# Retention and MLP-Mixer on one core: who picks the copy of an on-chip buffer

## The chip, the cores and the metric

One core of a Trainium2 chip runs the whole kernel in one launch. The metric is device microseconds, the median of several runs. Before the change it is 189.53 us (three runs, 188.84 to 191.23). On the chip, matmul operands are in float16, sums and the residual in float32; input and output are float32.

## The reference

The input is q, k and v of 4 batches, 8 heads, 768 steps and 64 channels, and four weights. A decayed linear attention comes first, and a mixer block on its output:

```python
state = gamma * state + k_t (outer) v_t          # per batch and head
y_t   = scale * q_t @ state
x     = y, heads side by side                    # 4 x 768 x 512
h     = relu(x^T @ w_tok1) @ w_tok2              # mixes the 768 steps, 256 wide
u     = x + h^T
out   = u + relu(u @ w_ch1) @ w_ch2              # mixes the 512 channels, 1536 wide
```

## The kernel before

The work is cut into operations (class `Op`), each a short run of instructions of one engine, about 1,300 in all. A **front** of a batch `b` and a pair of heads `p` (16 of them) does the attention and the token mixing. It loads q, k and v through POOL's queue (`load`, L494 and L497), scales k and q by the decay into the buffers `k16` and `q16` (`decayed`, L535 on ACT, L537 on DVE), and turns them to `kT` and `qT` (`turn`). In batches 0 and 1 the turning is done by TensorE (L559, L561); in batches 2 and 3 it is done by transposing DMAs of SP's queue (L549, and L785 for `uT`), which read `k16`, `q16` and `u16`. Then come the chunk states (L591, buffer `U` at L601 and L603, buffer `rz` at L621), the scores (L642), the masked scores `am` (L653), the outputs (L673, L699), the evacuation to `x16`, `u16` and `X` (L715), and the two token matmuls (L730, L750). A **back** of a batch widens to 1536 (`widen` L829, `widen7` L898) and narrows to 512 (`narrow` L974, `narrow7` L1048 and L1058). `widen7` and `narrow7` form seven products where eight would be the plain count; they keep partial sums in the buffer `us` (L909, L1038), which DVE adds later (L918, L1065), and sums of operands in `hs`. Output rows leave from `X` by SP's and ACT's queues (L989, L1091).

The **order** of every engine is a fixed list in the source (`ORDERED`), and so is the engine of each operation that could go to two (`WAYS`). The planner `arrange` walks these lists with a cost of each operation and a model of the DMA queues, and gives each operation a start. The program is written in the order of these starts. Three other things hang on the planned times: which of the 8 PSUM banks each accumulator gets, in what sequence the engines' streams are interleaved in the program, and how many filler matmuls (L1173, on zeros) TensorE runs in planned pauses before 21 us.

A buffer in SBUF has a number of copies (`BUFS`): 4 of k, q, v, `kT`, `qT` and `x16`, 3 of `k16`, `u16`, `rz` and `X`, 8 of `am`, 5 of `h1`, 2 of `q16`, `U`, `uT`, `h2`, `hs` and `us`, and one of `late`. An operation that opens a buffer (its `takes`) must wait until all users of the tile that had the copy before are done. Before the change, the planner lets such an operation wait for the oldest tile of the buffer, in the order of taking:

```python
q = taken[s.tag]
k = len(q) - BUFS[s.tag] + ...
x = slot_free(q[k])
```

but it doesn't say which copy is meant. The tile is asked for under the buffer's name with `bufs=BUFS[tag]`, and the allocator of the language picks a copy. Only `rz`, whose tiles are three standing constants, goes round in the order of writing (`made`). PSUM banks are chosen otherwise: the planner takes, of the banks that the operation may have, the one whose last tile is planned to be free first (`room`), and asks for it by its own name (`bank0` to `bank7`).

The planner's model of a transposing DMA, which a step below uses, has a first delay, 48 units and a landing:

```python
FIRST = dict(SP=600, POOL=1800, ACT=700)
return 1600 if t < 115000 else 900       # land(), for op.dma[0] == 48
..., [dst], [src], dma=(48, 28))         # turn(), mode "x"
```

Of the kernel before, what the change touches and what calls it, by code (L numbers as in the profile page):

```python
# [10 lines left out]
F16 = mybir.dt.float16  # L11
# [86 lines left out]
F_ON = 21000  # L98
# [2 lines left out]
FREE = dict(PE=300, ACT=2500, DVE=900, POOL=900, SP=750)  # L101


def arrange(ops, BUFS, BANKS, seq, ways):


    INF = 1e18
    n = len(ops)
    end, start, eng = [None] * n, [None] * n, [None] * n
    begun = [False] * n  # L110
    rings = Rings()
    free = dict(FREE)
    taken = {t: [] for t in BUFS}
    bank_slot = {i: None for i in range(8)}
    lanes, turns = [], []
    line = {e: [] for e in ENGINES}
    for i in seq:
        line[ops[i].ways[ways[i]][0]].append(ops[i])
    at = dict.fromkeys(ENGINES, 0)
    order = []  # L120
    tiled = ""
    t = 0.0

    def slot_free(s):
        m = 0
        for u in s.users:
            x = end[u.n]
            if x is None:
                return INF
            if x > m:  # L130
                m = x
        return m + SEM

    def ready(o, e):
        m = 0
        if o.behind is not None and not begun[o.behind.n]:
            return INF
        for d in o.after:
            x = end[d.n]
            if x is None:  # L140
                return INF
            if x > m:
                m = x
        for d in o.deps:
            if not begun[d.n]:
                return INF
            if end[d.n] is None:
                return INF
            if eng[d.n] == e and e == "PE":
                x = start[d.n]  # L150
            else:
                x = end[d.n] + (25 if eng[d.n] == e and d.dma is None else SEM) + o.guard
            if x > m:
                m = x
        return m

    def room(o):
        m, banks = 0, []
        for s in o.takes:
            if s.tag in BANKS:  # L160
                best = None
                for i in BANKS[s.tag]:
                    if i in banks or i == 7 and t < F_ON:
                        continue
                    x = 0 if bank_slot[i] is None else slot_free(bank_slot[i])
                    if best is None or x < best[0]:
                        best = (x, i)
                if best[0] >= INF:
                    return INF, None
                banks.append(best[1])  # L170
                m = max(m, best[0])
            else:
                q = taken[s.tag]
                k = len(q) - BUFS[s.tag] + sum(1 for s2 in o.takes[:o.takes.index(s)] if s2.tag == s.tag)
                if k >= 0:
                    x = slot_free(q[k])
                    if x >= INF:
                        return INF, None
                    m = max(m, x)
        return m, banks  # L180

    def lane(o, e):
        if o.dma is None or e == "POOL" or len(lanes) < 8:
            return 0
        x = end[lanes[-8].n]
        if x is None:
            return INF
        x += SEM
        if o.dma[0] == 48 and len(turns) > 2:
            y = end[turns[-3].n]  # L190
            if y is None:
                return INF
            x = max(x, y - 900)
        return x

    left = n
    while left:
        moved = False
        wake = INF
        for e in ENGINES:  # L200
            if free[e] > t:
                wake = min(wake, free[e])
                continue
            if at[e] >= len(line[e]):
                continue
            o = line[e][at[e]]
            r = ready(o, e)
            if r > t:
                wake = min(wake, r)
                continue  # L210
            m, banks = room(o)
            m = max(m, lane(o, e))
            if m > t:
                wake = min(wake, m)
                continue
            at[e] += 1
            way = o.ways[ways[o.n]]
            s_ = t
            if e == "PE":
                if o.tiled != tiled:  # L220
                    s_ = max(t, free[e] + (INTO if o.tiled else 0) + (OUT_OF if tiled == "high" else 0))
                tiled = o.tiled
            start[o.n], eng[o.n], begun[o.n] = s_, e, True
            free[e] = s_ + way[1]
            if o.dma:
                for d, x in rings.add(e, o, t):
                    end[d.n] = x
                if e != "POOL":
                    lanes.append(o)
                    if o.dma[0] == 48:  # L230
                        turns.append(o)
                if e == "SP":
                    free[e] = max(t + way[1], rings.made["SP"][-3])
            else:
                end[o.n] = s_ + way[2]
            for i, s in zip(banks, [s for s in o.takes if s.tag in BANKS]):
                bank_slot[i] = s
            for s in o.takes:
                if s.tag not in BANKS:
                    taken[s.tag].append(s)  # L240
            order.append((o, e, way, banks))
            left -= 1
            moved = True
            wake = min(wake, free[e])
        if moved:
            continue
        nxt = min(wake, rings.event)
        for d, x in rings.advance(nxt):
            end[d.n] = x
        if nxt >= INF:  # L250
            raise RuntimeError(f"the plan is stuck at {t}: {left} left")
        t = max(nxt, t + 1) if nxt <= t else nxt
    while rings.event < INF:
        for d, x in rings.advance(rings.event):
            end[d.n] = x
    for o, e, way, banks in order:
        for i, s in zip(banks, [s for s in o.takes if s.tag in BANKS]):
            s.bank = i
    return max(x for x in end), order, start, end

# [46 lines left out]
def kernel(  # L307
# [12 lines left out]
    B, H, S, D = q.shape  # L320
    P = 128
    NC = S // P
# [11 lines left out]
    const_p = ctx.enter_context(tc.tile_pool(name="const", bufs=1))  # L334
    sb = ctx.enter_context(tc.tile_pool(name="sb", bufs=1))
# [2 lines left out]

    BUFS = dict(late=1, k=4, q=4, v=4, k16=3, q16=2, kT=4, qT=4, U=2, r16=2, rz=3, am=8, X=3, x16=4, h1=5, u16=3,
                uT=2, h2=2, hs=2, us=2)  # L340
    BANKS = dict.fromkeys(("first", "front", "back", "back0", "last"), range(8))
    SEVEN = (0, 1, 2, 3)
    SPLIT = (0,)
    WIDE7 = (1, 2, 3,)
# [12 lines left out]
    ops = []  # L357

    def tile_of(slot, shape, dtype):
        if slot.tag == "rz":  # L360
            slot.tile = cross[made[0] % len(cross)]
            made[0] += 1
        elif slot.bank is not None:
            slot.tile = ps.tile(shape, dtype, name=f"bank{slot.bank}", bufs=1)
        else:
            slot.tile = sb.tile(shape, dtype, name=slot.tag, bufs=BUFS[slot.tag])
        return slot.tile


# [26 lines left out]
    ident16 = const_p.tile([P, P], F16, name="ident16")  # L396
    mask = const_p.tile([P, 1, P], FP, name="mask")
    zero = const_p.tile([P, 384], F16, name="zero")
    cross, made = [const_p.tile([P, NC - 1, 2, D], F16, name=f"cross{i}") for i in range(BUFS["rz"])], [0]
    g128 = [(1.0 - 2.0 ** (-5.0 - h)) ** P for h in range(H)]  # L400

    def prep(eng, cost, emit, deps=(), prio=(-20, 0, -1), takes=(), uses=()):
# [23 lines left out]
    def emit():  # L426
        nc.gpsimd.iota(tile_of(SINCE, [P, HC, P], FP), pattern=[[0, HC], [1, P]], base=-MID, channel_multiplier=0,
                       allow_small_or_imprecise_dtypes=True)
# [8 lines left out]
    def emit():  # L437
        gq = tile_of(LATE, [P, NP, SH], FP)
        for p in range(NP):
            nc.scalar.activation(gq[:, p], SINCE.tile.rearrange("p i t -> p (i t)"), AF.Exp, bias=lnsc, scale=lnh[:, p:p + 1])  # L440
# [668 lines left out]
    for what in ORDER:  # L1109
        n = int(what[1:2])  # L1110
# [7 lines left out]
        elif what[0] == "a":  # L1118
            f = CF[n]
# [36 lines left out]
    seq = [digit[a] * 62 + digit[c] for a, c in zip(ORDERED[::2], ORDERED[1::2])]  # L1156
    asked = set(o.n for o in queue)
    asked = [ops[i] for i in seq if i in asked]
    for i, o in enumerate(asked[6:]):
        o.after.append(asked[i])  # L1160
    total, order, start, end = arrange(ops, BUFS, BANKS, seq, [int(x) for x in WAYS])
    for o in ops:
        o.start, o.end = start[o.n], end[o.n]
    nc.vector.memset(zero, 0.0)
# [41 lines left out]
```

## Time and profile before

| | |
|---|---|
| median of three runs | 189.53 us (188.84 to 191.23) |
| the profiled execution | 188.35 us, of which the span of the instructions is 186.6 us |
| TensorE (PE) busy | 178.5 us, 96% of the span, 2093 matmuls |
| VectorE (DVE) busy | 169.6 us, 91%, 464 instructions |
| ScalarE (ACT) busy | 134.7 us, 72%, 306 instructions |
| GpSimd (POOL) busy | 53.7 us, 29%, 63 instructions (mostly issues of loads) |
| granted TensorE clock | full in all 40 slices but for rounding |

"Busy" is the time in which at least one instruction of the engine runs. The idle time before an instruction is put down to what released it. A row of a view by line names the engine, the line in the code, the tile written and the tiles read. Numbers of buffers are left out in these names, so that `k` there may be the loaded k or the buffer `k16` (the row `k<-k,gk` writes `k16` from k), and every PSUM bank is `bank`.

### The profile page before, as it was taken

What the parts mean: (1) busy time and instruction counts of PE and PEld (TensorE: products, weight loads), DVE (VectorE), ACT (ScalarE), POOL (GpSimd) and SP (SyncE); (2) the same over time, 40 slices, a digit from 0 to 9 for tenths busy, and PEclk for the clock granted to TensorE, in tenths of its full rate; (3) what the DMA queues carried; (4) which work ended last, traced back from release to release, by engine and by line L of the source; (5) the groups of instructions that cost most, each with busy time, mean ns of one, the idle gap of its engine ahead of it and who ended that gap; (6) DMA issues with size and microseconds to landing.
All of it is one profiled execution on the core that took longest, in us unless ns stands there. A gap on an engine that the chain in (4) does not pass through costs nothing.

```text
span 186.6 us, 5303 instructions
## 1 busy us (share of the span) xinstructions
PE 178.5 (96%) x2093; PEld 134.7 (72%) x2093; DVE 169.6 (91%) x464; ACT 134.7 (72%) x306; POOL 53.7 (29%) x63
## 2 busy tenths in 40 slices
PE   7888999999999999999999999999999999999990
PEld 3456888656779988866678899767678985566890
DVE  6599898979989998998999999999899999989981
ACT  5749898566899799999999798897983416562210
POOL 8995856544524606506040200000000000000000
PEclk9999999999999999999999999999999999999999
DMA  6999999999999999999999699270019136300053
GB/s 116 160 161 181 197 168 203 197 188 204 161 154 151 144 119 179 130 130 127 161 152 128 178 129 218 42 163 4 0 56 168 34 102 243 152 0 0 4 212 127
DMA packets 92249, 24.92 MB, mean 134 GB/s; under 512 B 81984, under 2 KB 89280, under 8 KB 92224
## 3 DMA queue, kind: packets, MB, share of 16 engines
q0 software_dynamic: 67728, 13.18, 92.7%
q1 hardware_dynamic: 23200, 9.57, 26.6%
q10 hardware_dynamic: 1296, 1.84, 3.2%
q8 instruction: 16, 0.26, 0.6%
q14 instruction: 9, 0.07, 0.1%
HBM read 26.74 MB, written 6.29 MB: 177 GB/s over the span
## 4 chain that ended last, share of the span: by engine, by line
PE 76%; DMA 8%; POOL 6%; ACT 5%; DVE 2%; issue 1%; POOLq 0%; ACTq 0%
PE bank L898 21%; PE bank L1048 14%; PE bank L1058 10%; PE bank L829 7%; PE bank L750 5%; DMA wt<-in_moe_w_tok_dram 4%; PE bank L730 4%; DMA kT<-k 3%; PE bank L642 3%; PE bank L974 3%; PE bank L673 2%; POOL v L497 2%; PE bank L699 2%; POOL k L497 2%; ACT h L845 1%; PE bank L795 1%
## 5 line engine op out<-in xcount | busy, mean ns | idle before, releaser
L653 DVE TENSOR_TENSOR am<-bank,mask 128x384 f16<-128x384 f32 x64 | 33.1, 553 | 2.2 <-PE bank L642 2.2
L918 DVE TENSOR_TENSOR h<-bank,us 128x384 f16<-128x384 f32 x54 | 29.0, 556 | 1.1 <-PE bank L898 0.7
L909 ACT COPY us<-bank 128x384 f32<-128x384 f32 x49 | 22.5, 485 | 9.2 <-PE bank L898 7.7
L497 POOL DMA_DIRECT2D v<-in_v_dram x16 | 16.4, 1023 | 38.9 <-PE bank L699 17.8
L898 PE MATMUL bank<-hs,late 128*128 128x384 f16 x108 | 22.3, 326 | 0.0
L1038 ACT COPY us<-bank 128x256 f32<-128x256 f32 x30 | 11.0, 374 | 14.6 <-PE bank L1048 12.8
L1048 PEld LDWEIGHTS <-hs 128*128 128x128 f16 x198 | 18.5, 98 | 2.5
L1065 DVE TENSOR_TENSOR X<-X,bank 128x256 f32<-128x256 f32 x44 | 17.7, 419 | 1.1 <-PE bank L1058 0.7
L898 PEld LDWEIGHTS <-late 128*128 128x128 f16 x144 | 13.0, 98 | 7.3 <-DVE hs L868 0.4
L621 ACT ACTIVATE cross<-U,gp 64x320 f16<-64x320 f32 x31 | 17.3, 560 | 1.1 <-DVE U L603 0.6
L829 PE MATMUL bank<-uT,wc 128*128 128x384 f16 x96 | 17.7, 326 | 0.0
L1048 PE MATMUL bank<-wsum,hs 128*128 128x256 f16 x132 | 17.6, 273 | 0.0
L497 POOL DMA_DIRECT2D k<-in_k_dram x15 | 15.3, 1022 | 7.9 <-ACT k L535 3.9
L603 DVE SCALAR_TENSOR_TENSOR U<-U,gp,bank 128x64 f32<-128x64 f32 x64 | 17.0, 278 | 0.6
L535 ACT ACTIVATE k<-k,gk 128x384 f16<-128x384 f16 x23 | 13.8, 623 | 3.7 <-DMA k<-in_k_dram 2.4
L845 ACT ACTIVATE h<-bank 128x384 f16<-128x384 f32 x24 | 11.1, 493 | 6.7 <-PE bank L829 6.5
L898 PE MATMUL bank<-uT,wc 128*128 128x384 f16 x72 | 15.8, 326 | 0.0
L715 ACT CAST u<-bank 128x384 f16<-128x384 f32 x32 | 15.1, 484 | 0.9 <-PE bank L750 0.8
L750 PE MATMUL bank<-h,wt 128*128 128x128 f16 x192 | 15.4, 219 | 0.1
L898 PEld LDWEIGHTS <-wc 128*128 128x128 f16 x108 | 10.1, 98 | 5.9 <-issue 0.4
L715 ACT CAST x<-bank 128x384 f16<-128x384 f32 x29 | 13.4, 488 | 0.9 <-PE bank L699 0.9
L1058 PEld LDWEIGHTS <-h 128*128 128x128 f16 x132 | 12.5, 98 | 1.8
(90 smaller groups left out, 390.6 us busy)
## 6 DMA issues: line engine op xcount, KB each, us to landing
out_dram<-X SPq DMA_DIRECT2D x17, 256.0 KB, 2.5
q<-in_q_dram POOLq DMA_DIRECT2D x16, 192.0 KB, 7.7
v<-in_v_dram POOLq DMA_DIRECT2D x16, 192.0 KB, 7.1
k<-in_k_dram POOLq DMA_DIRECT2D x15, 192.0 KB, 8.3
wc<-in_moe_w_ch_dram POOLq DMA_DIRECT2D x5, 512.0 KB, 13.3
out_dram<-X ACTq DMA_DIRECT2D x6, 256.0 KB, 2.2
wc<-in_moe_w_ch_dram POOLq DMA_DIRECT2D x2, 256.0 KB, 9.6
us<-in_k_dram SPq DMA_DIRECT2D x1, 384.0 KB, 3.6
```

The costliest lines, as they stand in the source:

```text
L497: (nc.sync if hard else nc.gpsimd).dma_start(out=tile_of(s, [P, 2, NC, D], FP if hard else F16), in_=src.rearrange("h (c p) d -> p (h c) d ...
L621: nc.scalar.activation(r, u, AF.Copy, scale=g)
L653: nc.vector.tensor_tensor(am, SC[g].tile[:, :m * P].rearrange("p (i t) -> p i t", t=P), mask.to_broadcast([P, m, P]), ALU.mult)
L715: (nc.scalar.copy if e == "ACT" else nc.vector.tensor_copy)(tile(), t)
L750: nc.tensor.matmul(Y[j].tile[:, 2 * i * D:2 * (i + 1) * D], wt2[:, jt, t], H1.tile[:, jt], start=False, stop=(jt == NJ - 1), skip_group_ch ...
L829: nc.tensor.matmul(acc[:, :SH], wc1[:, ct, ft * P:(ft + 1) * P], UT.tile[:, ct, sh * SH:(sh + 1) * SH], start=(ct == 0), stop=(ct == NP - 1))
L898: nc.tensor.matmul(acc[:, :SH], left(ct), r[:, ct], start=first and ct == 0, stop=ct == C2 - 1, skip_group_check=True)
L909: (nc.scalar.copy if e == "ACT" else nc.vector.tensor_copy)(ks[:, j], R1.tile[:, :SH])
L918: nc.vector.tensor_tensor(h(m, sh), R.tile[:, :SH], KS.tile[:, j], ALU.add)
L1048: nc.tensor.matmul(acc_[:, lo], l[:, j], r[:, j], start=first and j == 0, stop=j == K2 - 1, skip_group_check=True)
L1058: nc.tensor.matmul(acc_[:, lo], l[:, j], r[:, j], start=first and j == 0, stop=j == K2 - 1, skip_group_check=True)
L1065: (nc.vector if e == "DVE" else nc.gpsimd).tensor_tensor(dst(), dst(), b_(), ALU.add)
```

## The change

Each copy of each SBUF buffer gets an identity of its own beside the banks: `BANKS` now maps every buffer to a range of numbers from 8 up. The planner chooses among them by the rule of the banks, the copy that it plans to be free first, in place of the wait for the oldest tile. The tile is asked for by a name of its own (`k16_21`, say) with one copy, so nothing is left to the allocator. The three tiles of `rz` are picked by the same number instead of going round. The lists of order and of engines, and all operations, stay as they are.

```diff
-def arrange(ops, BUFS, BANKS, seq, ways):
+def arrange(ops, BANKS, seq, ways):
...
-    taken = {t: [] for t in BUFS}
-    bank_slot = {i: None for i in range(8)}
+    bank_slot = {i: None for ids in BANKS.values() for i in ids}
...
         for s in o.takes:
-            if s.tag in BANKS:
-                best = None
-                for i in BANKS[s.tag]:
...
-            else:
-                q = taken[s.tag]
-                k = len(q) - BUFS[s.tag] + sum(1 for s2 in o.takes[:o.takes.index(s)] if s2.tag == s.tag)
-                if k >= 0:
-                    x = slot_free(q[k])
-                    if x >= INF:
-                        return INF, None
-                    m = max(m, x)
+            best = None
+            for i in BANKS[s.tag]:
+                if i in banks or i == 7 and t < F_ON:
+                    continue
+                x = 0 if bank_slot[i] is None else slot_free(bank_slot[i])
+                if best is None or x < best[0]:
+                    best = (x, i)
+            if best[0] >= INF:
+                return INF, None
+            banks.append(best[1])
+            m = max(m, best[0])
...
-    BANKS = dict.fromkeys(("first", "front", "back", "back0", "last"), range(8))
+    BANKS, ids = dict.fromkeys(("first", "front", "back", "back0", "last"), range(8)), 8
+    for tag, n in BUFS.items():
+        BANKS[tag], ids = range(ids, ids + n), ids + n
...
         if slot.tag == "rz":
-            slot.tile = cross[made[0] % len(cross)]
-            made[0] += 1
-        elif slot.bank is not None:
+            slot.tile = cross[slot.bank - BANKS["rz"][0]]
+        elif slot.bank < 8:
             slot.tile = ps.tile(shape, dtype, name=f"bank{slot.bank}", bufs=1)
         else:
-            slot.tile = sb.tile(shape, dtype, name=slot.tag, bufs=BUFS[slot.tag])
+            slot.tile = sb.tile(shape, dtype, name=f"{slot.tag}_{slot.bank}", bufs=1)
```

More of the change, by code (lines that the diff above doesn't have):

```diff
@@ L159, in room @@
         for s in o.takes:
-            if s.tag in BANKS:
-                best = None
-                for i in BANKS[s.tag]:
[L163 to L168, printed above, removed]
-                    return INF, None
-                banks.append(best[1])
-                m = max(m, best[0])
-            else:
-                q = taken[s.tag]
-                k = len(q) - BUFS[s.tag] + sum(1 for s2 in o.takes[:o.takes.index(s)] if s2.tag == s.tag)
-                if k >= 0:
-                    x = slot_free(q[k])
-                    if x >= INF:
-                        return INF, None
-                    m = max(m, x)
+            best = None
[9 more added lines that the diff above has]
+            m = max(m, best[0])
         return m, banks
@@ L235, in arrange @@
                 end[o.n] = s_ + way[2]
-            for i, s in zip(banks, [s for s in o.takes if s.tag in BANKS]):
+            for i, s in zip(banks, o.takes):
                 bank_slot[i] = s
-            for s in o.takes:
-                if s.tag not in BANKS:
-                    taken[s.tag].append(s)
             order.append((o, e, way, banks))
@@ L256, in arrange @@
     for o, e, way, banks in order:
-        for i, s in zip(banks, [s for s in o.takes if s.tag in BANKS]):
+        for i, s in zip(banks, o.takes):
             s.bank = i
@@ L398 @@
     zero = const_p.tile([P, 384], F16, name="zero")
-    cross, made = [const_p.tile([P, NC - 1, 2, D], F16, name=f"cross{i}") for i in range(BUFS["rz"])], [0]
+    cross = [const_p.tile([P, NC - 1, 2, D], F16, name=f"cross{i}") for i in range(BUFS["rz"])]
     g128 = [(1.0 - 2.0 ** (-5.0 - h)) ** P for h in range(H)]
@@ L1160 @@
         o.after.append(asked[i])
-    total, order, start, end = arrange(ops, BUFS, BANKS, seq, [int(x) for x in WAYS])
+    total, order, start, end = arrange(ops, BANKS, seq, [int(x) for x in WAYS])
     for o in ops:
```

## The prediction

> **What bounds the kernel now.** I read the page's first part, then the windows (busy time of each engine by stretch), then who TensorE waited for, then the chain that ended last, and last the timeline around the one wait for a copy that this chain goes through.
>
> ```profile
> span 186.6 us, 5303 instructions
> PE 178.5 (96%) x2093; PEld 134.7 (72%) x2093; DVE 169.6 (91%) x464; ACT 134.7 (72%) x306; POOL 53.7 (29%) x63
> ```
>
> ```profile
> core 0: us, PE busy (x) PEld busy (x) DVE busy (x) ACT busy (x) POOL busy (x), PEclk, DMA share, GB/s
> 0.00:20.00 20.00, 16.98 (x220) 10.21 (x221) 15.73 (x65) 14.13 (x26) 16.51 (x24) 1.00 1.65 158
> 20.00:58.00 38.00, 37.70 (x506) 28.49 (x506) 34.47 (x76) 29.72 (x69) 21.39 (x25) 1.00 1.84 182
> 58.00:78.00 20.00, 19.88 (x302) 17.53 (x301) 18.91 (x52) 18.69 (x44) 8.07 (x9) 1.00 2.16 144
> 78.00:98.00 20.00, 19.82 (x215) 13.21 (x213) 19.37 (x59) 19.07 (x46) 6.68 (x7) 1.00 2.02 142
> 98.00:120.00 22.00, 21.79 (x293) 19.02 (x291) 21.90 (x61) 19.84 (x48) 1.01 (x1) 1.00 1.02 143
> 120.00:165.00 45.00, 44.98 (x426) 32.93 (x421) 42.77 (x112) 28.24 (x67) 0.00 (x0) 1.00 0.37 98
> 165.00:182.30 17.30, 17.30 (x150) 13.31 (x148) 16.07 (x44) 5.00 (x12) 0.00 (x0) 1.00 0.18 66
> 182.30:186.60 4.30, 0.04 (x1) 0.00 (x0) 0.42 (x1) 0.00 (x0) 0.00 (x0) 0.98 0.28 105
> ```
>
> TensorE sets the time. From 20.0 to 182.3 us it is idle for 0.30 + 0.12 + 0.18 + 0.21 + 0.02 = 0.83 us in all (length less PE busy, row by row). The 3.0 us before 20 us are a wait for first loads, and the 4.3 us behind 182.3 us are the last add and its transfer. Among what TensorE waited for after 20 us no line has more than 0.2 us:
>
> ```profile
> PE bank L591 <- ACT uT L801: 0.2, 1, 0.2
> PE bank L1048 <- DVE h L918: 0.2, 1, 0.2
> PE bank L898 <- DVE h L918: 0.2, 1, 0.2
> ```
>
> A busy PE could still be a slow one. The chain's long pieces answer that (start, length, matmuls):
>
> ```profile
> 124.32 2.65 PE bank L898 x16
> ...
> 134.05 2.60 PE bank L898 x16
> ...
> 154.01 10.99 PE bank L898 x66
> ```
>
> These are 166, 163 and 167 ns a matmul of 384 columns: the same pace wherever one follows the other, so inside the pieces there is nothing to win, and only the seams between them hold more. One more row of the windows, for the last of these pieces (PE busy, then PEld busy):
>
> ```profile
> 154.00:165.00 11.00, 11.00 (x68) 6.36 (x66) 10.45 (x26) 6.78 (x15) 0.00 (x0) 1.00 0.44 168
> ```
>
> The Trainium skill (Perfetto Trace Analysis, "Identifying the Most-Contended Engine") says that matmul busy time does not tell how far TensorE is from its roofline, and that the share of weight loads should be read instead. By that rule the 72% of PEld would leave over a quarter of the span open, and copies that come free earlier could take some of it. The trace does not bear it out here: from 154.01 to 165.00 us matmuls run at 167 ns each without a gap, though weight loads fill 6.36 of these 11.00 us. What this rule would give is the third rival below.
>
> **The change part by part.** No instruction is added, removed or moved to another engine, and each engine's order stays. So every term is a wait that changes its end, or a bank that changes its number.
>
> *Copies whose last reader is always one engine.* The last readers of `v` and `am` are L673 on PE, of `x16` L730, of `h1` L750, of `kT` L642, of `qT` and `rz` L699, all on PE; of `us` they are adds on DVE (L918, L1065); of `U` the scaling at L621, on ACT but for one. One engine's order is fixed, so these copies come free in the same order in the plan and on the chip, whatever the clock. The first planned to be free is then the first that is free. The waits for copies that the trace shows are of this sort:
>
> ```profile
> POOL v L497 <- PE bank L699: 17.8, 4, 5.9
> POOL v L497 <- PE bank L673: 9.9, 2, 9.2
> ...
> ACT us L1038 <- DVE X L1065: 1.8, 1, 1.8
> ...
> ACT us L909 <- DVE h L918: 0.8, 2, 0.5
> ```
>
> Behind POOL's wait for `v` stand the later loads of q, k and v, but TensorE waits for no load after 20 us (rows above). These 27.7 us are hidden by TensorE's work; without that cover, a late load would show as a PE wait at L591. ACT's waits for `us`, 2.6 us, hold up ACT's next evacuations. The copy waited for is the first to come free already, so I take 0 for all of these; bounds: −2.6 if I am wrong about `us` and all of it is on the path, and 0 above, since a copy freed in fixed order can't be picked later.
>
> *Copies with readers on several engines.* These are `k16`, `q16`, `u16`, k and q: in batches 2 and 3 a transposing DMA is among the last readers. One such take waited badly:
>
> ```profile
> 52.74 0.62 ACT k L535
> ...
> 58.62 6.17 DMA kT<-k
> 65.06 0.35 issue
> 65.41 0.35 ACT us L1038
> ```
>
> ```profile
> 57.43 0.32 DVE L537 TENSOR_SCALAR k<-k,gk 128x384 f16<-128x384 f16 x1
> ...
> 60.47 0.51 PE L591 MATMUL bank<-v,k 128*64 128x64 f16 x20
> ...
> 61.19 0.31 DVE L537 TENSOR_SCALAR k<-k,gk 128x384 f16<-128x384 f16 x1
> ...
> 64.89 0.62 ACT L535 ACTIVATE k<-k,gk 128x384 f16<-128x384 f16 x1 [1.18 <-DMA kT<-k]
> ...
> 65.58 0.23 PEld L642 LDWEIGHTS <-kT 64*128 64x128 f16 x8 [0.21 <-issue]
> ...
> 66.10 0.15 PEld L642 LDWEIGHTS <-kT 64*128 64x128 f16 x4 [0.30 <-issue]
> ```
>
> `k16` has three copies, opened at 52.74, 57.43 and 61.19. The next take, at 64.89, waited 1.18 us for the DMA that reads the second, though the first, of batch 1 and read by PE alone, had its last reader end at 60.98 (the row at 60.47). The allocator gave it the wrong one. Which one will the plan give? By the constants of its model a transposing DMA lands 0.60 + 48 × 0.028 + 1.60 = 3.5 us after its issue if nothing else moves, so 62.2 us at the earliest here, and later under POOL's loads. That is behind 60.98, so the plan should take the first copy, and the wait of 1.18 us goes away. Queued behind it on ACT are the `us` evacuation at 65.41 and others that TensorE wants; what TensorE shows of it are the two pauses of its weight loads, 0.21 + 0.30 = 0.51 us, and little idle time of its own. Bounds: 0 and −1.18 us. I take −0.3, nearer to the 0.12 us that PE is idle from 58 to 78 us. DVE is late next: it is busy 18.91 of 20 us there and 21.90 of 22 us from 98 on, so part may be given back.
>
> *Banks dealt anew.* Where the old rule waits for the oldest tile and another is free earlier, the planned times move, by little, and from there on the banks may be dealt out otherwise. A bank dealt badly costs TensorE the rest of an eviction:
>
> ```profile
> L653 DVE TENSOR_TENSOR am<-bank,mask 128x384 f16<-128x384 f32 x64 | 33.1, 553 | 2.2 <-PE bank L642 2.2
> L918 DVE TENSOR_TENSOR h<-bank,us 128x384 f16<-128x384 f32 x54 | 29.0, 556 | 1.1 <-PE bank L898 0.7
> ```
>
> The old deal leaves TensorE 0.83 us of idle time, so the bounds are −0.8 and, for four bad takes at a whole eviction, 4 × 0.556 = +2.2 us. The rule that deals them is unchanged, hence 0.
>
> *Start, end, addresses.* In the first 20 us nearly every copy is used for the first time, so no choice differs, and the 3.0 us and the fillers stay:
>
> ```profile
> L1173 PE MATMUL bank<-zero 128*128 128x384 f16 x35 | 9.1, 400 | 1.1 <-DVE zero L1164 1.1
> ```
>
> If a start did shift, a filler fewer or more is hidden by the wait for loads. The tail's 4.3 us has no copy to wait for. Other addresses cost 0: 64 writes of `am` into eight copies differ by 21 ns at most:
>
> ```profile
> L653 DVE TENSOR_TENSOR am<-bank,mask x64: 544/552/565, 8.8 to 135.2; 128x384 f16<-128x384 f32 x64
> ```
>
> **Sum.** 186.6 − 0.3 = 186.3 us of span. The profiled execution took 188.35 us, 1.75 us more than its span, so it would take 188.05. The median of the three runs is 189.53, 1.18 us above the profiled execution, and on that scale I predict 189.53 − 0.3 = **189.2 us**. That is no change by the measure of 2% (3.8 us), about what a measurement of this kernel can tell.
>
> **The rivals.**
>
> *Nothing moves at all (189.5 us).* The plan picks what the allocator picked, at 64.89 us too. For it: nearly all orders of release are fixed. Against it: the wait of 1.18 us, which the plan's own constants avoid.
>
> *Slower: the plan trusts its landing times.* The copies read by transposing DMAs are freed in the plan by a model (3.5 us alone, 2.8 us after 115 us). The trace has, from issue to landing:
>
> ```profile
> kT<-k SPq DMA_TRANSPOSE x8, 5.5
> qT<-q SPq DMA_TRANSPOSE x8, 3.4
> uT<-u SPq DMA_TRANSPOSE x8, 3.1
> ```
>
> For `k16` the chip is up to 2.0 us later than the model alone. If the plan then hands out a copy that a DMA still reads, ACT or DVE stands at the head of its queue, evacuations behind it are late, and TensorE finds no bank. Priced by the one such wait shown, 1.18 us, all of it on the path, it decides (3.8 us) from the fourth time on: 189.53 + 4.72 = 194.3 us; three times give 193.1. Against it: such a wait cost TensorE far less than 1.18 us here, and under POOL's loads the model slows these DMAs as well.
>
> *Faster: the copies' waits were all on the path.* The waits for copies on ACT are 1.18 + 1.8 + 0.8 = 3.8 us; if all go and TensorE gains all, 189.5 − 3.8 = 185.7 us. Against it: TensorE's idle time is 0.83 us.
>
> **How the numbers follow.** Forecast 0.50, nothing moves 0.20, slower rival 0.22 (0.17 of it beyond 2%), faster rival 0.08 (0.06 beyond). So faster 0.06, within 2% 0.77, slower 0.17. The range goes down by the visible idle time and the whole `k16` wait, 189.53 − 0.83 − 1.18 = 187.5, and up to three bad takes, 189.53 + 3.54 = 193.1; that leaves out the far part of both outer rivals.
>
> **What would show it.** Right: the wait of ACT L535 for the DMA `kT<-k` is gone, POOL's waits for `v` are as long as before, PE is idle under 1 us from 20 us on, fillers are the same 35 and the last matmul ends near 182 us. Wrong: new waits of ACT or DVE for `DMA kT<-k`, `qT<-q` or `uT<-u` at L535, L537 or L715, PE waits for L653 or L918 of half a microsecond, or PE idle time in a stretch that had none; or a start that differs in its first 20 us.

## The result and the profile after

The changed kernel takes 189.04 us (median of 20 runs, 187.73 to 190.72), the kernel before, run beside it, 190.0 us (20 runs, 188.73 to 191.29). The ratio is 0.9938, with a 95% interval from 0.9912 to 0.9965: faster by 0.6%, or 1.2 us (0.7 to 1.7). By the measure of 2% this is no change.

Read side by side, the two programs have the same instructions in the same order on every engine, the same 35 fillers, and the same bank for each of the 268 accumulators. The differences are 30 of the 64 takes of `am`, which exchange copies, two neighbouring takes of `k16`, the addresses, and one more semaphore instruction of ACT. (Lines of the kernel after are 12 lower from `load` on: L535 is L523, L549 is L537, L642 is L630, L898 is L886.)

The page's head and the windows of the profile after, with the same columns as before:

```profile
span 187.8 us, 5304 instructions
PE 178.1 (95%) x2093; PEld 134.7 (72%) x2093; DVE 170.2 (91%) x464; ACT 134.5 (72%) x306; POOL 53.6 (29%) x63
```

```profile
58.00:78.00 20.00, 19.41 (x298) 17.20 (x296) 18.94 (x54) 19.16 (x45) 8.55 (x9) 1.00 2.09 139
78.00:98.00 20.00, 19.14 (x206) 12.63 (x205) 18.93 (x55) 17.59 (x43) 6.11 (x7) 1.00 1.95 141
98.00:120.00 22.00, 21.79 (x290) 19.20 (x288) 21.90 (x62) 19.87 (x49) 1.37 (x2) 1.00 1.06 149
120.00:165.00 45.00, 44.99 (x434) 33.01 (x432) 42.84 (x113) 28.68 (x69) 0.00 (x0) 1.00 0.37 98
```

The faster kernel has the longer span here, 187.8 us against 186.6. One execution is a draw: this one took 189.6 us, above its median, and the profile of before was of an execution of 188.35 us, well below its own. So the two can't be subtracted, and the sections below read each wait in several executions.

The wait for a copy is gone. ACT's timeline around it, after:

```profile
62.98 0.61 ACT L523 ACTIVATE q<-q,gy 128x384 f16<-128x384 f16 x1
63.50 0.46 ACT L703 COPY X<-bank 128x384 f32<-128x384 f32 x1
63.86 0.61 ACT L523 ACTIVATE k<-k,gk 128x384 f16<-128x384 f16 x1
64.38 0.36 ACT L1026 COPY us<-bank 128x256 f32<-128x256 f32 x1
65.29 0.38 ACT L727 ACTIVATE h<-bank 128x256 f16<-128x256 f32 x1 [0.55 <-PE bank L718]
```

The scaling of k follows at once, and ACT now waits for TensorE a little later instead (0.55 us at L727): it has run ahead. The waits for `v` and `us` are as before:

```profile
POOL v L485 <- PE bank L687: 18.0, 4, 6.5
...
POOL v L485 <- PE bank L661: 10.1, 2, 9.1
...
ACT us L1026 <- DVE X L1053: 1.8, 1, 1.8
...
ACT us L897 <- DVE h L906: 0.8, 2, 0.5
```

What made this execution long are two losses that the profile of before did not have:

```profile
76.83 0.51 PE L630 MATMUL bank<-qT,kT 64*128 64x128 f16 x12 [0.59 <-DMA kT<-k]
...
87.22 0.81 DVE L525 TENSOR_SCALAR q<-q,gy 128x384 f16<-128x384 f16 x1 [0.84 <-DMA qT<-q]
...
88.54 0.81 PE L886 MATMUL bank<-hs,late 128*128 128x384 f16 x4 [0.47 <-DVE h L906]
```

At 76.8 us the scores wait until a turned k has landed. At 87.2 us DVE waits to write a copy of `q16` that a transposing DMA still reads; the add behind it in DVE's queue is late, and TensorE waits for its bank.

### The profile page after: what moved, and what is told of

The parts are those of the page before. It is cut to its first block, busy times and chain, and to the rows that moved or that the text cites. A ratio compares the mean times of both kernels' runs of the same rounds, so it can differ in the third digit from the quotient of the medians.

```text
span 187.8 us, 5304 instructions
## 1 busy us (share of the span) xinstructions
PE 178.1 (95%) x2093; PEld 134.7 (72%) x2093; DVE 170.2 (91%) x464; ACT 134.5 (72%) x306; POOL 53.6 (29%) x63
## 4 chain that ended last, share of the span: by engine, by line
PE 74%; DMA 9%; ACT 7%; POOL 5%; DVE 3%; issue 1%; POOLq 0%
PE bank L886 20%; PE bank L1036 13%; PE bank L1046 10%; PE bank L817 7%; PE bank L738 5%; DMA v<-in_v_dram 5%; PE bank L718 5%; DMA kT<-k 4%; PE bank L962 3%; PE bank L630 2%; PE bank L661 2%; POOL k L485 2%; POOL v L485 2%; PE bank L579 2%; PE bank L687 1%; ACT h L833 1%
## 5 line engine op out<-in xcount | busy, mean ns | idle before, releaser
L886 PE MATMUL bank<-hs,late 128*128 128x384 f16 x108 | 22.5, 326 | 0.5 <-DVE h L906 0.5
L886 PEld LDWEIGHTS <-late 128*128 128x128 f16 x144 | 13.0, 98 | 8.0 <-issue 0.9
L886 PE MATMUL bank<-uT,wc 128*128 128x384 f16 x72 | 15.8, 326 | 0.0
L523 ACT ACTIVATE k<-k,gk 128x384 f16<-128x384 f16 x23 | 13.7, 618 | 2.2 <-DMA k<-in_k_dram 2.1
L886 PEld LDWEIGHTS <-wc 128*128 128x128 f16 x108 | 10.1, 98 | 6.1 <-issue 0.6
```

The costliest lines, as they stand in the source:

```text
L886: nc.tensor.matmul(acc[:, :SH], left(ct), r[:, ct], start=first and ct == 0, stop=ct == C2 - 1, skip_group_check=True)
```

## The experiments

### Which part of the change it is

Every ratio here is to the kernel before, run beside the kernel in question, with its 95% interval. Two kernels split the change. In the first, only `k16` is named and chosen by the plan:

```diff
-            slot.tile = sb.tile(shape, dtype, name=f"{slot.tag}_{slot.bank}", bufs=1)
+            own = slot.tag == "k16"
+            slot.tile = (sb.tile(shape, dtype, name=f"{slot.tag}_{slot.bank}", bufs=1) if own else
+                         sb.tile(shape, dtype, name=slot.tag, bufs=BUFS[slot.tag]))
```

> Only k16 is taken from the change: its three copies are named and chosen by the plan, all other buffers are left to the allocator as before. Against the kernel before, two takes of k16 swap copies (the one that waited 1.18 us for the transposing DMA and the next one) and nothing else moves. Theory (this one take is the whole gain): ratio 0.994, between 0.991 and 0.997, ACT's wait for DMA kT<-k at the scaling line is gone. Rival (the gain comes from the new addresses of all copies or from the 30 takes of am that differ): ratio 1.000, though that wait is gone.

Measured: 0.9956 (0.9924 to 0.9987), and the scaling of k (L525 in both of these kernels) follows without a wait:

```profile
64.29 0.61 ACT L525 ACTIVATE k<-k,gk 128x384 f16<-128x384 f16 x1
```

The second has `own = slot.tag != "k16"`.

> The change without k16: all other copies are named and chosen by the plan, k16 is left to the allocator, which gives the take at 64.9 us the same copy as before. Theory (the k16 take is the whole gain): ratio 1.000, between 0.997 and 1.003, and the ACT wait of about 1.2 us for DMA kT<-k is back. Rival (addresses or am): ratio 0.994.

Measured: 1.0016 (0.9989 to 1.0043), and the wait is back in its profile, shorter than in the profile of before:

```profile
65.86 0.62 ACT L525 ACTIVATE k<-k,gk 128x384 f16<-128x384 f16 x1 [0.72 <-DMA kT<-k]
```

So addresses and the 30 takes of `am` are worth nothing that can be measured, and the choice of a copy for `k16` is worth the gain, as far as these intervals can tell. A third kernel gets the same without any naming: the kernel before, with `k16=4` in place of `k16=3`.

> The kernel before, with a fourth copy of k16 and the allocator as before. 13 of 16 takes get another copy, none of them one that a DMA still reads. Theory (the wait for the copy, not who names it, is what counts): ratio 0.994, the same as the change, and no ACT wait for DMA kT<-k. Rival (the plan's names or addresses count): ratio 1.000.

Measured: 0.9932 (0.9906 to 0.9958), without an ACT wait for `DMA kT<-k`. Who names the copy does not matter; that no DMA still reads it does.

### More copies of other buffers

The wait at 87.2 us above is for one of two copies of `q16`. The changed kernel with `q16=3`:

> The changed kernel with a third copy of q16; banks, order and everything else are as in the changed kernel. In the profile after, DVE waits 0.8 us at the scaling of q for DMA qT<-q, near 86 us, for one of the two copies, and TensorE is 0.63 and 0.2 us later after it than in the profile before. Theory (takes that wait for a transposing DMA are what is left): that wait is gone and the ratio to the kernel before is 0.991, so 0.003 below the change alone. Rival (what follows is late anyway since the turned q itself lands late): the wait is gone and the ratio stays at 0.994.

Measured: 0.9927 (0.9902 to 0.9952), with no wait of DVE for `DMA qT<-q`. That is the lowest ratio of all, but its interval holds the change alone (0.9938), so whether the third copy of `q16` adds to it is not settled. The same third copy in the kernel before:

> The kernel before with a third copy of q16, k16 left as it was, with its bad take. The profiles show 0.15 to 0.5 us of TensorE's time for the bad take itself, and the change gained about 1 us, so half a microsecond is not yet found. In two of ten profiles a turned q landed late, near 87 us, DVE waited for a copy of q16 until then, and TensorE lost 0.85 us. Theory (the bad take makes such a late landing more frequent, and that is the rest): ratio to the kernel before 0.997, and no loss near 88 us in its profile. Rival (that event has nothing to do with it and is rare): 1.000.

Measured: 0.9986 (0.9959 to 1.0013). The interval holds both expectations. Its profile has the bad take (one of a copy that a transposing DMA still reads), 1.2 us of wait, and no loss near 88 us.

A third copy of `us`, with a third of `q16`, paid for by `x16=2` and `h1=2`:

> The changed kernel with a third copy of q16 and a third of us, paid for by two copies of x16 in place of 4 and two of h1 in place of 5. Order, banks and fillers are the same. ACT's waits for us at the evacuations (1.8 and 0.8 us in both profiles) should go. Theory (what TensorE waits for after 20 us are no longer copies of us): ratio to the kernel before 0.992, the same as with the third q16 alone, though these waits are gone. Rival (they are on the path): 0.986 or below. If x16 or h1 are now short: above 0.995, with new waits of ACT at their evacuations.

Measured: 0.9959 (0.9932 to 0.9986). No gain from it is seen. The wait of 0.8 us is gone, but the longer of the two waits that were to go is still there:

```profile
ACT us L1026 <- DVE X L1053: 1.8, 1, 1.8
```

So this wait was never for a copy of `us`; the prediction had read it as one. ACT's timeline in this kernel shows what it is:

```profile
178.37 0.34 ACTq L977 DMA_DIRECT2D out_dram<-X  x1
178.75 0.37 ACT L1026 COPY us<-bank 128x256 f32<-128x256 f32 x1 [1.77 <-DVE X L1053]
```

ACT's queue has to issue an output transfer first, whose last add on DVE ended at 178.33 us, and the evacuation follows. The kernel before has the same pair at 176.93 and 177.31 us. The ratio lies above 0.995, where the expectation put it if `x16` or `h1` were short, but the waits that would go with that are not there: ACT's waits at their evacuations are all for TensorE's banks. The interval also holds the change alone (0.9938).

### What a bad take costs

The kernel before, unchanged, has four more profiles (its second to fifth), and the kernel after a second one.

> The kernel before, unchanged, profiled once more. Its first profile is one of its fastest executions (188.35 us against a median near 190), so the wait of 1.18 us in it may be a short one. Theory (the wait lasts until the transposing DMA lands, which differs from execution to execution, and TensorE pays what exceeds about 0.85 us): the wait of ACT for DMA kT<-k near 65 us is 1.0 to 2.5 us here, and TensorE's stretch from 800th to 850th matmul, 4.39 us in the first profile and 4.05 without the wait, is 4.05 plus the wait less 0.85. Rival (the wait is always about 1.2 us and the rest of the 1.0 us gained comes from elsewhere): 1.1 to 1.3 us, stretch 4.4.

> The changed kernel, unchanged, profiled once more. In its first profile two stretches were long that no copy of k16 explains: TensorE waited for DMA kT<-k at 76 us (+0.66 us) and was late again at 88 us (+0.85 us). Theory (these are late transposing DMAs of that execution): at least one of them is gone here. Rival (the change causes them): both are there again. ACT's wait for DMA kT<-k near 64 us is absent under both.

> The kernel before once more, as in the other look at it. Theory: wait of ACT for DMA kT<-k between 0.5 and 2.5 us, and not the same as in the two other profiles; TensorE's stretch from the 800th to the 850th matmul follows it, 4.05 plus the wait less 0.85. Rival: 1.1 to 1.3 us again, 4.4.

> The kernel before, unchanged, one more profile. Theory: the wait of ACT for DMA kT<-k is 0.7 to 1.5 us, and TensorE loses the wait less 0.85 us where it is behind it, 0.14 us shortly after, and in some executions 0.4 us near 76 and 0.85 us near 88 us. Rival: no loss beyond the first two.

> As the look before it: one more profile of the kernel before, with the same two expectations.

The waits of ACT for `DMA kT<-k` in the second to the fifth profile of the kernel before:

```profile
ACT k L535 <- DMA kT<-k: 1.0, 1, 1.0
```

```profile
ACT k L535 <- DMA kT<-k: 0.9, 1, 0.9
```

```profile
ACT k L535 <- DMA kT<-k: 0.5, 1, 0.5
```

```profile
ACT k L535 <- DMA kT<-k: 0.6, 1, 0.6
```

What TensorE pays is seen at its next scores. In the first profile of before, then in the second profile of after (each row has start, length, and at its end the number of matmuls):

```profile
65.58 0.84 PE L642 MATMUL bank<-qT,kT 64*128 64x128 f16 x12
66.36 1.49 PE L1048 MATMUL bank<-wsum,hs 128*128 128x256 f16 x12
```

```profile
65.76 0.51 PE L630 MATMUL bank<-qT,kT 64*128 64x128 f16 x12
66.20 1.48 PE L1036 MATMUL bank<-wsum,hs 128*128 128x256 f16 x12
```

From the scores to the next group it is 0.78 us with the wait and 0.44 without it: 0.34 us lost. The table does this for every matmul. It compares the times from start to start with those of the second profile of after, and gives what is longer by over 0.06 us (times in us; the last matmul is the 2093rd; the run is the sum of the two columns behind it and 6.3, within 0.04).

| kernel, its profile | run | start of the 226th matmul | from there to the last | ACT waits for `DMA kT<-k` | TensorE longer, at |
|---|---|---|---|---|---|
| before | 188.35 | 20.45 | 161.62 | 1.2 | 0.34 at 66; 0.16 at 68 to 71 |
| before, profile 2 | 188.84 | 20.86 | 161.69 | 1.0 | 0.23 at 34; 0.20 at 66; 0.15 at 68 to 71 |
| before, profile 3 | 189.17 | 21.64 | 161.24 | 0.9 | 0.15 at 68 to 71 |
| before, profile 4 | 189.23 | 21.85 | 161.10 | 0.5 | none |
| before, profile 5 | 188.66 | 21.00 | 161.37 | 0.6 | 0.25 at 29 |
| before with three `q16` | 189.28 | 21.09 | 161.89 | 1.2 | 0.25 at 29; 0.37 at 66; 0.15 at 68 to 71 |
| all but `k16` | 190.48 | 21.90 | 162.31 | 0.7 | 0.36 at 76; 0.85 at 87 to 89 |
| after | 189.60 | 20.74 | 162.58 | none | 0.66 at 76; 0.85 at 87 to 89 |
| after, profile 2 | 188.03 | 20.65 | 161.09 | none | (reference) |
| `k16` only | 188.56 | 21.15 | 161.14 | none | none |
| four `k16` | 189.50 | 22.11 | 161.11 | none | none |
| after with three `q16` | 188.42 | 20.73 | 161.43 | none | 0.32 at 34 |
| three `us` | 189.80 | 22.23 | 161.28 | none | 0.19 at 29 |

In these profiles a bad take costs TensorE nothing at waits of 0.5 to 0.7 us. From 0.9 us on it costs the wait less about 0.85 us, and some 0.15 us a little later. The first theory of these profiles, with its 0.85 us, holds. Its range of waits, up to 2.5 us, was too wide: 0.5 to 1.2 us was seen. The range for the fourth and fifth profile, from 0.7 us on, missed both (0.5 and 0.6), and neither has the losses near 76 and 88 us that were expected in some. The rival's 1.1 to 1.3 us was missed each time. The two losses at 76 and 87 us occur with the good take and with the bad one, and are both absent from the second profile of after, so the choice for `k16` doesn't cause them. Whether the rest of the change makes them more frequent is open: they are in two of the six profiles of kernels in which the copies of all other buffers are named, the last kernel below among them, and in none of the eight of kernels that leave these to the allocator. A third of the six, with three `us`, has landings of `kT` and `qT` nearly as late at these places (9.1 and 8.1 us against 10.5 and 8.9) without a loss.

Over the seven profiles with the bad take the mean loss at 66 to 71 us is 0.22 us (0.50, 0.35, 0.15, 0, 0, 0.52, 0). The timed runs say 1.2 us (0.7 to 1.7). A last kernel puts plain work of ACT in the place of the wait: the changed kernel, with

```diff
             slot.tile = sb.tile(shape, dtype, name=f"{slot.tag}_{slot.bank}", bufs=1)
+            if slot.tag == "k16":
+                nth[0] += 1
+                if nth[0] == 11:
+                    for _ in range(2):
+                        nc.scalar.activation(idle, zero, AF.Copy, scale=gk[:, 0:1])
```

> The changed kernel, in which ACT does two scalings of zeros into a spare tile (2 x 0.52 us from start to start) right before the take of k16 that waited 1.18 us before the change. The wait is replaced by work of a like length that no DMA can stretch. The bad take is the cause by the one-change experiments, which is worth 0.6% (1.1 us), but the profiles show only 0 to 0.5 us of it on TensorE. Theory 1 (1 us of ACT time here costs TensorE 0.2 plus 0.14 us, as in the profiles, and the rest of the gain comes with longer or further waits for the DMA): ratio to the kernel before 0.996. Theory 2 (a delay of ACT here costs the whole of it in most executions): ratio 1.000.

Measured: 0.9986 (0.9959 to 1.0013). Its profile has the work in the place of the wait, 1.17 us from its start to that of the scaling:

```profile
65.30 1.27 ACT L359 ACTIVATE idle<-zero,gk 128x384 f16<-128x384 f16 x2
66.47 0.60 ACT L529 ACTIVATE k<-k,gk 128x384 f16<-128x384 f16 x1
```

TensorE loses 0.20 us at its next scores and 0.16 us a little later, as with a wait of 1.0 us. The ratio's interval just reaches theory 1 (0.996) and holds theory 2 (1.000). So most of the gain is given back by a delay of ACT at this one place, which agrees with where it came from. Here too the timed runs pay more than the profile shows: 0.9 us by the two ratios (0.9986 against 0.9938), 0.36 us in the profile.

**What stays open.** Of the gain of about 1.2 us, the profiles account for 0 to 0.5 us by the wait itself. The rest, some half a microsecond or more, is shown by the timed runs alone. The start doesn't hold it: the 226th matmul begins at 21.3 us on average in the seven profiles with the bad take and in the six without. The choice of profiles may hide some of it, as all five profiles of the kernel before are of executions (188.35 to 189.23 us) below the medians of their series (189.5 to 189.6). One candidate is that in executions without a kept profile the DMA lands later still; the kernel with ACT held speaks against it, as its delay has a fixed length and the timed runs pay more than its profile all the same. Another is that the losses at 76 and 87 us come more often where ACT is late. One profile in seven with the bad take has these losses and one in six without it, which decides nothing.

## Why the prediction was right, point by point

*TensorE sets the time, and little can be won.* Right. In the second profile of after, TensorE is idle for 0.40 us in all from 58 us to 165 us (0.00, 0.36, 0.04 and 0.00):

```profile
58.00:78.00 20.00, 20.00 (x308) 17.84 (x307) 19.32 (x54) 19.16 (x44) 8.55 (x9) 1.00 2.19 150
78.00:98.00 20.00, 19.64 (x210) 13.00 (x208) 19.70 (x60) 19.04 (x47) 6.39 (x7) 1.00 1.84 138
98.00:120.00 22.00, 21.96 (x296) 19.17 (x296) 21.89 (x61) 19.76 (x48) 1.01 (x1) 1.00 0.97 142
120.00:165.00 45.00, 45.00 (x420) 32.88 (x419) 42.75 (x112) 28.09 (x68) 0.00 (x0) 1.00 0.36 98
```

Where the prediction said "PE is idle under 1 us from 20 us on", the profile after breaks it, with 0.59 + 0.86 us from 58 to 98 us, by late DMAs, which the kernel without the new choice for `k16` has too; its last matmul starts at 183.3 us, not near 182.

*Copies freed by one engine: 0.* Right for the time: their orders came out as argued, but for 30 takes of `am`, and POOL's waits for `v` are 18.0 + 10.1 us against 17.8 + 9.9. One row was misread: ACT's 1.8 us at the evacuation to `us` is a wait for an output transfer's rows and not for a copy, as the kernel with three copies shows, so the bound of −2.6 and the faster rival's 3.8 us counted 1.8 us that no copy could give.

*`k16`: −0.3, bounds 0 and −1.18.* The mechanism was right to the take: the plan hands out the copy that TensorE has done with, and the kernels with `k16` alone, without `k16` and with four of it show that this is the gain. The size is the step that failed: the term was put at −0.3 us and measured −1.2 us (−0.7 to −1.7) in the timed runs. It was sized by the two pauses in one execution, 0.51 us, which in the table are 0.50 us for just that execution; the median of runs paid more than this profile, one of the fastest, could show. Why they paid more stays open, as said above. That DVE would give part of it back is not seen.

*Banks dealt anew: 0.* The number was right, the picture wrong: the prediction let the planned times move and the banks with them, but not one bank differs.

*Nothing moves at all.* Ruled out: the wait is gone in both profiles of the change, and the interval of the ratio ends below 1.

*Slower rival.* It did not come about: no take of the changed kernel waits for a DMA that the old one did not wait for. Its mechanism is real, though: a copy still read by a transposing DMA is what the old kernel waits for at 64.9 us, and both wait for at `q16`. The profile of before has that second wait too, so the wait of 1.18 us was not "the one such wait shown":

```profile
DVE q L537 <- DMA qT<-q: 0.5, 1, 0.5
```

The lateness of the DMAs was also read too small: 5.5 us is the middle one of eight landings of `kT`, and the DMA of the bad take itself took 6.17 us, 2.6 us more than the model's 3.5 and not "up to 2.0".

That 189.53 − 0.3 = 189.2 comes so near to the measured 189.04 is luck: the kernel before was measured 0.5 us slower in the longer series (190.0), and the term was 0.9 us too small. From 190.0 the same forecast would have been 189.7.

## What to carry to other kernels

When several engines and queues free the copies of a buffer, check at each take which copy is given and who reads it last; a copy held by a DMA can cost a wait while another stands free, and one more copy cures it as well as a better choice. Look at what the engine that sets the time loses behind such a wait, not at its length: 0.5 to 0.7 us of ACT's wait cost TensorE nothing in these profiles, and 1.2 us cost 0.5. But one profile can price it too low, as it did here: the timed runs paid 1.2 us. And a gain below 1% can't be read from one profile of each kernel; split the change into kernels and time those.

## What the runs showed of the hardware that was not expected

The spread of the runs lies mostly in the start. The 226th matmul begins between 20.45 and 22.23 us in the thirteen profiles of the table, while the time from there to the last one, the losses at 76 and 87 us aside, keeps within 161.1 to 161.9 us.

The time from issue to landing of the transposing DMAs varies widely. In the profile after, for all of `kT` and `qT`:

```profile
DMA to landing us min/median/max: 2.7/4.7/10.5
```

The Trainium skill (DMA: Bandwidth & Descriptors, "Issuing engines are not separate DMA queues") says that DMAs of different issuing engines run on the same 16 DMA engines and interleave. The trace agrees as far as it goes: the longest of them, issued at 72.78 us, has three loads of POOL's queue issued from 70.50 us on beside it, and the shortest, at 104.07 us, none.

```profile
70.50 1.02 POOL L485 DMA_DIRECT2D v<-in_v_dram  x1 [5.33 <-PE bank L687]
71.51 1.03 POOL L485 DMA_DIRECT2D q<-in_q_dram  x1
72.51 1.04 POOL L485 DMA_DIRECT2D k<-in_k_dram  x1
```

The loads beside a DMA don't explain all of it. These are the same DMA of the same program, in the first and in the second profile of after:

```profile
69.73 2.37 SPq L537 DMA_TRANSPOSE kT<-k  x1
```

```profile
69.65 1.21 SPq L537 DMA_TRANSPOSE kT<-k  x1
```

The first landed 7.1 us after its issue, and is what the scores at 76.8 us waited for; the second landed after 3.0 us. The three loads next issued by POOL start at 70.43, 71.44 and 72.44 us in the second profile, within 0.1 us of the times above. What made the first one late is not shown.
